# Joint key and value weight loads, token runs of four rows and a newly searched order in a linear-attention and gated-MLP kernel

## The chip, the cores and the metric

The kernel runs on 1 core of one Trainium2 chip. The metric is the time of one execution in microseconds (us) on the device. Executions of one program differ by 0.5 to 3.5 us here, so every comparison below uses several executions and, in the experiments, executions of the kernel before in the same rounds on the same chip. "Span" is the length of the profiled execution as the profile sees it, some 2 us less than the time.

## The reference, cut to what matters

Four layers act on 2048 tokens of 512 values: linear attention, gated MLP, linear attention, gated MLP. Both attentions use the same weights.

```python
def _A_ref(x, wqkv, w_phi, wo):                 # B, S, D = 1, 2048, 512;  H = 32, Dh = 16
    q, k, v = ...                               # x @ wqkv, by heads
    pq = einsum("bhsd,hdf->bhsf", q, w_phi); pk = einsum("bhsd,hdf->bhsf", k, w_phi)
    phi_q = concat([softmax(pq), softmax(-pq)]); phi_k = concat([softmax(pk), softmax(-pk)])
    kv = einsum("bhsf,bhsd->bhfd", phi_k, v);  z = phi_k summed over s
    o = (phi_q @ kv) / (phi_q . z + 1e-6)
    return o.reshape(B, S, D) @ wo
def _B_ref(x, W_gate, W_up, W_down): ...        # relu gate, F = 1376
x = x + _A_ref(layernorm(x), ...);  x = x + _B_ref(layernorm(x), ...)   # and both once more
```

Each attention sums over all tokens (kv, z) before any token can go on. So the kernel has a front, which ends with the first kv product, and a second part. The matrix of the feature map is multiplied into the key weights once ("composed") so that keys come out ready for the softmax.

## The kernel before

The program is a list of operations, each with the tiles that it reads and writes. A table ORDER gives the sequence of operations on each engine and a table CHOICE the engine of those that can run on several. Both were found by a search outside of the kernel. Each engine executes its list strictly in order.

```python
# warm-up: 70 matmuls on a tile of ones, spread by ORDER over the gaps of the first 19 us
for j in range(NWARM):
    op("pe", lambda e: e.matmul(k.pb[3][:, 0:128], k.ones[:], k.ones[:], start=True, stop=True), ...)

# the first loads: 128 KB each, value weights and key weights apart, four token tiles
for ic in range(NC):
    dma("act", ... k.wv_p[:, ic, :] <- A_wqkv[ic * 128:(ic + 1) * 128, 1024:1536])
for ic in range(NC):
    dma("act", ... wk_n[:, ic, :] <- A_wqkv[ic * 128:(ic + 1) * 128, 512:1024])
for t in range(4):
    ldx(t, t + 1)
dma("sp", ... k.phi_c[:] <- A_w_phi)            # the feature map
first = [r("x", 3)]                             # the large loads wait for token tile 3
ldx(4, 8, first); ldx(8, 12, first); ldx(12, 16, first)
...                                             # [cut]
# the end of the front: the kv product is masked and copied out
op("dve", lambda e: e.tensor_tensor(k.kvbd..., pv..., k.mask4..., ALU.mult), ...)   # "kvbd"
```

The softmax here doesn't subtract the row's maximum and nothing guards it: scores larger than these inputs give would overflow.

## Time and profile before

| | before |
|---|---|
| time, median of 3 runs | 379.60 us (379.32 to 379.97) |
| span of the profiled run | 377.4 us |
| statistics of the group of token tile 4 begin | 10.99 us |
| first kvbd copies begin (end of the front) | 53.07 us |
| second kvbd copies begin (third layer) | 236.32 us |

The last three rows are the milestones. From the first kvbd on TensorE is full: its idle time after 50 us, summed over the bracketed waits in its timeline, is 1.2 us. The time is the front, plus the stretch between the two kvbd copies (183.25 us), plus the rest (141.1 us). Three more rows of the timeline of the kernel before (start, duration, engine, line, operation, tiles, count):

```profile
7.60 0.81 PE L725 MATMUL ps<-wv_p,yT 128*128 128x512 bf16 x3
10.99 2.46 DVE L623 BATCH_NORM_STATS2 stats<-x_sb 128x6 f32<-128x512 bf16 x4
6.05 1.48 SPq L543 DMA_DIRECT2D x_sb<-in_A_x_dram  x3
```

The first value projection runs at the fast pitch (three matmuls of 512 columns in 0.81 us). VectorE begins the statistics of the large token group at 10.99. SyncE issues the three large token loads at 6.05, when tile 3 has landed.

### The profile page before, as it was taken

How to read it: one execution, taken by the hardware profiler on the slowest of the kernel's cores; microseconds unless marked ns; L12 is line 12 of the kernel's file. 1: busy time of each engine (PE TensorE's matmuls, PEld its weight loads, DVE VectorE, ACT ScalarE, POOL GpSimd, SP SyncE). 2: the span in 40 equal slices, each digit the busy share in tenths (PEclk: the TensorE clock that was granted, in tenths of full speed). 3: DMA queues.
4: the chain of work that ended last, by engine and by line, in shares of the span. 5: the costliest groups of instructions: out<-in, count | busy, mean ns of one | idle time of the engine just before them, and what ended most of it. 6: DMA issues, size and time to landing. Idle time of an engine off the chain costs nothing.

```text
span 377.4 us, 6882 instructions
## 1 busy us (share of the span) xinstructions
PE 367.7 (97%) x2519; PEld 203.9 (54%) x2565; DVE 276.2 (73%) x607; ACT 227.0 (60%) x463; POOL 130.8 (35%) x234
## 2 busy tenths in 40 slices
PE   6999999999999999999999999999999999999997
PEld 5654555877744454454444446577664454445443
DVE  5999998989968676459799999898984654342323
ACT  3999878765744127874677568584635451653450
POOL 6799941133344001350463577023221201000020
PEclk9999999999999999999999999999999999999999
DMA  7632794313326444310300045335543442142012
GB/s 233 173 76 52 187 240 149 77 33 56 78 43 94 97 64 84 70 30 14 70 2 1 2 81 95 79 63 95 83 83 75 81 86 56 28 71 70 30 42 70
DMA packets 87856, 29.33 MB, mean 78 GB/s; under 512 B 79792, under 2 KB 86800, under 8 KB 87824
## 3 DMA queue, kind: packets, MB, share of 16 engines
q1 hardware_dynamic: 84368, 25.86, 33.7%
q10 hardware_dynamic: 3456, 3.05, 2.5%
q8 instruction: 20, 0.33, 0.4%
q14 instruction: 12, 0.10, 0.1%
HBM read 7.91 MB, written 2.10 MB: 27 GB/s over the span
## 4 chain that ended last, share of the span: by engine, by line
PE 85%; POOL 7%; DVE 3%; issue 2%; ACT 1%; DMA 1%; POOLq 0%; DVEq 0%
PE ps L962 37%; PE ps L1011 20%; PE ps L725 7%; PE ps L942 7%; POOL expk L750 5%; PE ps L822 5%; PE ps L988 3%; PE ps L921 2%; PE ps L787 1%; PE ps L886 1%; DMA hT<-in_A_wqkv_dram 1%; DVE Zk L744 1%; POOL rstd L648 1%; PE ps L868 1%; PE ps L539 0%
## 5 line engine op out<-in xcount | busy, mean ns | idle before, releaser
L962 PE MATMUL ps<-yT,Wgu 128*128 128x512 bf16 (+2 forms) x870 | 150.8, 320 | 0.6
L962 PEld LDWEIGHTS ps<-yT,Wgu 128*128 128x128 bf16 x880 | 78.5, 98 | 58.8 <-ACT expk L970 1.0
L964 ACT ACTIVATE gate_sb<-ps 128x512 bf16<-128x512 f32 (+2 forms) x110 | 50.7, 480 | 55.1 <-PE ps L962 41.8
L1011 PE MATMUL ps<-Wd,hT 128*128 128x512 bf16 (+4 forms) x354 | 79.3, 373 | 0.5
L1011 PEld LDWEIGHTS ps<-Wd,hT 128*128 128x128 bf16 (+1 forms) x363 | 34.6, 98 | 39.5 <-DVE hT L972 0.7
L972 DVE TENSOR_TENSOR hT<-gate_sb,expk 128x512 bf16<-128x512 bf16 (+2 forms) x70 | 23.9, 361 | 30.4 <-ACT expk L970 21.4
L970 ACT ACTIVATE expk<-ps 128x512 bf16<-128x512 f32 (+2 forms) x70 | 32.0, 475 | 22.2 <-PE ps L962 19.5
L710 ACT ACTIVATE sq<-x_sb,nmr 128x512 bf16<-128x512 bf16 x48 | 34.6, 721 | 10.3 <-DVE x_sb L687 6.6
L744 DVE TENSOR_REDUCE Zk<-expk 128x64 f32<-128x1024 bf16 x32 | 38.1, 1203 | 1.0 <-ACT expk L737 0.7
L714 POOL TENSOR_TENSOR rstd<-rv,mone 128x1 f32<-128x1 f32 x32 | 18.6, 589 | 50.2 <-DVE rv L712 50.0
L1013 DVE SCALAR_TENSOR_TENSOR x_sb<-ps,rstd,x_sb 128x512 bf16<-128x512 f32 (+2 forms) x33 | 23.9, 728 | 16.1 <-PE ps L1011 13.5
L942 PE MATMUL ps<-wo_p,oT 128*128 128x512 bf16 x118 | 30.8, 379 | 0.6 <-DVE oT L413 0.3
L975 DVE TENSOR_TENSOR hT<-gate_sb,ps 128x512 bf16<-128x512 bf16 (+2 forms) x40 | 21.7, 544 | 12.6 <-ACT gate_sb L964 6.4
L855 POOL TENSOR_TENSOR expq<-expq,rho 128x256 bf16<-128x256 bf16 x36 | 22.2, 624 | 24.4 <-DVE rho L852 23.7
L847 DVE TENSOR_REDUCE Zq<-expq 128x64 f32<-128x1024 bf16 x24 | 28.8, 1204 | 0.8 <-POOL rho L852 0.5
L687 DVE SCALAR_TENSOR_TENSOR x_sb<-ps,x_sb 128x512 bf16<-128x512 f32 x32 | 21.9, 687 | 8.6 <-PE ps L942 7.8
L750 POOL TENSOR_TENSOR expk<-expk,rZk 128x1024 bf16<-128x1024 bf16 x13 | 25.9, 2005 | 0.6 <-DVE rZk L746 0.6
L755 POOL TENSOR_TENSOR expk<-expk,rZk 128x512 bf16<-128x512 bf16 x17 | 19.1, 1134 | 11.8 <-DVE rZk L746 11.5
L822 PE MATMUL ps<-Wqp,yT 128*128 128x512 bf16 x91 | 22.8, 379 | 0.3
L725 PE MATMUL ps<-Wkp,yT 128*128 128x512 bf16 x84 | 22.0, 379 | 0.2
L725 PE MATMUL ps<-wv_p,yT 128*128 128x512 bf16 x85 | 21.9, 379 | 0.2
L712 POOL TENSOR_SCALAR rv<-rv 128x1 f32<-128x1 f32 x22 | 4.3, 203 | 45.3 <-ACT sq L710 45.3
(126 smaller groups left out, 514.1 us busy)
## 6 DMA issues: line engine op xcount, KB each, us to landing
out_dram<-x_sb ACTq DMA_DIRECT2D x15, 128.0 KB, 1.7
x_sb<-in_A_x_dram SPq DMA_DIRECT2D x3, 512.0 KB, 5.0
Wgu<-in_B_W_up_dram SPq DMA_DIRECT2D x4, 344.0 KB, 5.5
Wgu<-in_B_W_gate_dram SPq DMA_DIRECT2D x4, 344.0 KB, 4.3
Wd<-in_B_W_down_dram SPq DMA_DIRECT2D x5, 256.0 KB, 3.3
yT<-ytile SPq DMA_TRANSPOSE x56, 2.5
qT<-expq SPq DMA_TRANSPOSE x40, 2.5
x_sb<-in_A_x_dram SPq DMA_DIRECT2D x4, 128.0 KB, 3.6
```

The costliest lines, as they stand in the source:

```text
L710: op("act", lambda e: e.activation(k.sq[:], k.x_sb[:, t, :], ACT.Square, scale=-float(D), bias=k.nmr[:, t, :], accum_out=k.rv1[:, t, :]), ...
L725: op("pe", (lambda ic, bank, W: lambda e: e.matmul(k.pb[bank][:], k.yT[:, ic, t * 128:(t + 1) * 128], W[:, ic, :], start=(ic == 0), stop=( ...
L744: op("dve", lambda e: e.tensor_reduce(k.Zk[:, zb, :], k.expk[:, t, :, :, :].rearrange("p g s (h f) -> p (g s h) f", f=16), AX.X, ALU.add), ...
L750: op("pool", lambda e: e.tensor_tensor(kv, kv, k.rZk[:, rb, :].unsqueeze(2).to_broadcast([P, 64, 16]), ALU.mult), [r("expk", t, 0), r("exp ...
L822: op("pe", (lambda ic, bank, tt: lambda e: e.matmul(k.pb[bank][:], k.yT[:, ic, tt * 128:(tt + 1) * 128], k.Wqp[:, ic, :], start=(ic == 0), ...
L847: op("dve", lambda e: e.tensor_reduce(k.Zq[:, b, :], k.expq[:, t, :, :, :].rearrange("p g s (h f) -> p (g s h) f", f=16), AX.X, ALU.add), ...
L942: op("pe", (lambda c, bank: lambda e: e.matmul(k.pb[bank][:], k.oT[:, ob, c, :], k.wo_p[:, c, :], start=(c == 0), stop=(c == NC - 1)))(c, ...
L962: op("pe", (lambda bank, W, ic, fc, Mf: lambda e: e.matmul(k.pb[bank][0:Mf, 0:n], W[:, ic, fc * 128:fc * 128 + Mf], k.yT[:, ic, c0:c0 + n] ...
L964: op("act", (lambda Mf, gb, gs: lambda e: e.activation(k.gate_sb[0:Mf, gs, 0:n], k.pb[gb][0:Mf, 0:n], ACT.Relu))(Mf, gb, gs), [self.RP[gb] ...
L970: op("act", (lambda Mf, ub, up: lambda e: e.activation(up[0:Mf, 0:n], k.pb[ub][0:Mf, 0:n], ACT.Copy))(Mf, ub, up), [self.RP[ub]], ru, 170 ...
L972: op("dve", (lambda Mf, up, gs, u: lambda e: e.tensor_tensor(k.hT[0:Mf, u, 0:n], k.gate_sb[0:Mf, gs, 0:n], up[0:Mf, 0:n], ALU.mult))(Mf, u ...
L1011: op("pe", (lambda fc, Kf, u, c0, bank, m0, m1: lambda e: e.matmul(k.pb[bank][:, m0:m1], k.hT[0:Kf, u, c0:c0 + 128], k.Wd[0:Kf, fc, m0:m1] ...
```

## The change

Its intent: fewer and larger loads at the start (four weight loads of 256 KB in rows of 2 KB in place of eight of 128 KB in rows of 1 KB), the feature map multiplied into the loaded key weights in place, large token loads in packets of 4 KB since each partition holds four neighbouring rows, both queues used for the first tokens, and an order and choice searched for the new loads. All of ORDER and CHOICE differ. They are cut here.

```diff
 ORDER = { ... }      # [cut: every list is new]
 CHOICE = { ... }     # [cut: many small operations change their engine]
-        sb("wv_p", [NC, 512])
+        sb("wkv", [NC, 1024])
+        self.Wkp, self.wv_p = self.wkv[:, :, 0:512], self.wkv[:, :, 512:1024]
-        for ic in range(NC):
-            dma("act", ... k.wv_p[:, ic, :], A_wqkv[ic * 128:(ic + 1) * 128, 1024:1536] ...)
-        for ic in range(NC):
-            dma("act", ... wk_n[:, ic, :], A_wqkv[ic * 128:(ic + 1) * 128, 512:1024] ...)
-        for t in range(4):
-            ldx(t, t + 1)
-        dma("sp", ... k.phi_c ...)
+        def ldkv(eng, ic):
+            dma(eng, ... k.wkv[:, ic, :], A_wqkv[ic * 128:(ic + 1) * 128, 512:1536] ...)
+        ldx("sp", 0, 1)
+        ldx("act", 1, 2)
+        dma("sp", ... k.phi_c ...)
+        ldkv("act", 0)
+        ldkv("act", 1)
+        ldx("sp", 2, 3)
+        ldx("act", 3, 4)
+        ldkv("sp", 2)
+        ldkv("act", 3)
         first = [r("x", 3)]
-        ldx(4, 8, first) ...
+        ldx("sp", 4, 8, first) ...
-        WT, Wn = k.hT[:, 0:4, :], k.hT[:, 8:12, :]
+        WT, Wn = k.hT[:, 0:4, :], k.Wkp
+    def tokens(self, ap, t):
+        g = t // 4
+        v = ap.rearrange("b s d -> (b s) d")[512 * g:512 * g + 512, :]
+        return v.rearrange("(t p) d -> p t d", p=P) if g == 0 else v.rearrange("(p t) d -> p t d", t=4)
```

The stores use tokens() too.

## The prediction

> **What bounds the kernel now.** I read the page first (shares and slices), then the chain of waits, then the windows and the timeline of the first 60 us, because the diff touches the loads at the start.
>
> ```profile
> PE 367.7 (97%) x2519; PEld 203.9 (54%) x2565; DVE 276.2 (73%) x607; ACT 227.0 (60%) x463; POOL 130.8 (35%) x234
> PE   6999999999999999999999999999999999999997
> DVE  5999998989968676459799999898984654342323
> PE 85%; POOL 7%; DVE 3%; issue 2%; ACT 1%; DMA 1%; POOLq 0%; DVEq 0%
> ```
>
> The page says that TensorE bounds everything. For the second part that is true. For the first 53 us I don't take it at its word: the busy time there is full of filler. The timeline of TensorE has 70 matmuls on the tile of ones (the warm-up, L539), spread through the first 19 us in gaps. Real matmuls of 512 columns run at 1.73 us for 8, that is 216 ns each ("160.47 1.73 PE ps L725 x8" in the chain), those of 68 columns at some 33 ns (40 in 1.70 less the tail), those of 128 columns at 56 ns. By these pitches and the matmul counts in the program, the matmuls up to the last of the first key-value accumulation are 46.5 us (3.9 of them warm-up), but that one ends at 53.5. All matmuls together are 364.5 us, so 318.0 come after it; TensorE ends them near 374.4, so they lose about 2.9 us to gaps. The front loses 7.0, plus the 3.9 of filler. So the change can gain in the front, and hardly anywhere else.
>
> Who holds the front? The windows view (busy us in each stretch) and the DVE rows of the timeline:
>
> ```profile
> 2.00:4.00 2.00, 1.47 (x15) 1.20 (x14) 0.42 (x1) 1.21 (x2) 1.55 (x5) 1.00 0.88 286
> 4.00:6.00 2.00, 2.00 (x21) 2.00 (x20) 1.86 (x6) 0.60 (x1) 1.35 (x7) 1.00 0.97 288
> 6.00:8.00 2.00, 1.70 (x19) 1.27 (x19) 1.11 (x4) 0.60 (x1) 0.97 (x4) 1.00 0.87 273
> 8.00:10.00 2.00, 1.09 (x14) 0.68 (x13) 1.88 (x6) 0.94 (x2) 1.83 (x5) 1.00 1.04 352
> ...
> 3.50:8.35 4.85, 4.26 (x39) 3.48 (x40) 3.74 (x10) 1.19 (x2) 2.72 (x12) 1.00 0.92 283
> 8.35:53.10 44.75, 43.37 (x361) 23.94 (x366) 44.13 (x72) 42.05 (x65) 40.30 (x51) 1.00 0.62 136
> ```
> ```profile
> 3.58 0.69 DVE L623 BATCH_NORM_STATS2 stats<-x_sb 128x6 f32<-128x512 bf16 x1 [3.58 <-DMA x_sb<-in_A_x_dram]
> 6.94 0.69 DVE L623 BATCH_NORM_STATS2 stats<-x_sb 128x6 f32<-128x512 bf16 x1 [0.85 <-DMA x_sb<-in_A_x_dram]
> 8.35 0.41 DVE L413 COPY yT<-ps 128x512 bf16<-128x512 bf16 x1
> 16.31 1.22 DVE L744 TENSOR_REDUCE Zk<-expk 128x64 f32<-128x1024 bf16 x1 [0.22 <-ACT expk L737]
> 53.07 0.98 DVE L797 TENSOR_TENSOR kvbd<-ps,mask 128x136 bf16<-128x136 f32 x4
> ```
>
> From 8.35 to 53.1 us VectorE is busy 44.13 of 44.75 us (99%), ScalarE 42.05 (94%), GpSimd 40.30 (90%). The three are balanced, VectorE ahead. The chain names GpSimd's key scaling (L750), but only since the three hand over to each other. The masked copy of the key-value product (kvbd, 53.07) ends this phase and releases the part where TensorE is full. So the front ends when VectorE's list ends: landing of the first token tile (3.58), plus work, plus idle. Idle after 3.58: 1.11 us up to 8.35 (0.85 of it waiting for token tile 2) and 0.62 later. That 1.7 us is nearly all that better loading can win on VectorE, since the 3.58 stays.
>
> [...] the loads of 2 to 8 us (1 KB packets) move 273 to 288 GB/s, but those of 8 to 12 us, 1 KB packets too, 352 to 362. So 1 KB alone isn't the brake. [...] issues cost 0.43 to 0.46 us each on both queues while the engines are already 87 to 97% busy. [...]
>
> **The change part by part.**
> (1) Joint loads: eight weight loads of 128 KB become four of 256 KB: four issues fewer, 4 x 0.45 = 1.8 us of issuing; ScalarE's last weight issue comes at 4.52 now, and near 2.6 (five back to back from 0.80). The bytes (1 MB weights, 0.5 MB tokens, 16 KB feature map) stay. [...]
> (2) Order and split of queues: tokens 0 and 1 head the two queues, so both land near 3.6; tile 2 is third on SyncE behind the tiny map load. Some 0.55 MB are before its end: 2.1 us of start, 0.55 MB / 0.288 = 1.9, and 0.6 of completion (fitted on tile 0): near 4.7 to 5.5. VectorE reaches it after 2.0 us of its list, at 5.6: the wait of 0.85 goes. Tile 3 comes fourth on ScalarE's queue behind 512 KB of weights, with 1.3 MB moved: 2.1 + 4.4 + 0.6 = 7.1, later than now (about 6.0). VectorE wants it near 6.7, so 0.4 us of new wait. The large token loads wait on tile 3, so they start 1 us later[...].
> (3) Moves between engines in the front. VectorE gains two copies of 0.42, one of 0.69, and two small ones of 0.2 each (1.9); it loses two copies of 0.42, the block-diagonal map 0.68 and one token scaling of 0.48 (2.0). The clearing of kvf, 1.06 us on GpSimd, goes to VectorE in the time before 3.58: free. Net -0.1. ScalarE: three of 0.60 out, two of 0.60 and one of 0.81 in: +0.2. GpSimd: kvf and two small ones out, the map in: about -0.3.
> (4) Key weights: the map overwrites the loaded copy. The copies are ordered by the composition itself, so no wait is added. With all weights in near 8.0 us the first exponential could start near 13.5 instead of 15.01, which removes the 0.22 at 16.31 and gives ScalarE slack of over 1 us against +0.2 of work.
> (5) Stores: still rows of 1 KB per partition, now 4 KB apart in memory; same number and size, no change.
> (6) The same 364.5 us of matmuls; the new order after 53 us can only touch the 2.9 us of gaps there. Its 51 moves from GpSimd to VectorE and 33 back are of small pieces in a part where VectorE has room.
> Sum for VectorE's list: idle 1.7 becomes about 0.4 + 0.2 + 0.5 = 1.1, gain 0.6; less work 0.1; so the front ends some 0.7 us earlier, all of which reaches the end, as TensorE is full from there. For the search I add 0.4 in the later gaps, a choice and not a result. 379.6 - 1.1 = 378.5 us.
>
> **The rivals.**
> (a) Loading was hidden: VectorE is at 99%, so taking away its early wait only uncovers the next (tile 3, the large loads, or GpSimd). For it: tile 3 and all that hangs on it come later. Then 379.4 to 380.
> (b) The early phase is really bound by the composed key weights: 15.01 for the first exponential, with TensorE on filler until 14. Then joint loads win 1.5 us in the front for all three engines and the result is near 377.5. Against it: ScalarE starts its exponentials just in time for VectorE (only 0.22 of wait).
> (c) The feature map's 512 packets of 32 bytes, now second in SyncE's queue[...], hold tile 2 and the third weights back by up to 2 us. For it: 653 packets under 512 B pass in 4 to 8 us now, where the rate falls to 138 to 270 GB/s. Then VectorE idles as before and the time is 379.5 to 380.5.
> (d) Larger packets speed the token loads so that later tiles run freely: bounded by the 1.7 us of idle; 377.7.
>
> **Range and chances.** (a) and (c) are about 25% together, (b) and (d) about 30%, the rest about my sum. Beyond 2% would be below 372.0, a gain of 7.6 us: more than all of the front's 7.0 of gaps, so nearly excluded; slower by 2% (387.2) would need a stall that the order tables, made for these loads, don't suggest. The three runs of before span 0.65 us. Range 377.2 to 379.8; faster 0.01, within 2% 0.98, slower 0.01.
>
> **What would show it.** Right: VectorE's first statistics still near 3.6; no wait of 0.85 before the third; a short one before the fourth; kvbd at 52.0 to 52.7 instead of 53.07; the same TensorE time after it. Wrong: VectorE's first start later than 3.8, or kvbd not moved though the waits are gone (then GpSimd or ScalarE sets the end), or the gain arising after 53 us (then the search, not the loads, is the cause). Were the first exponential 1.5 us earlier and kvbd too, rival (b) was right.

Passages on the cost of a packet and on how the queues share the DMA engines are cut, since no trace of this case shows them. The sum came to 1.1 us: 0.6 less idle time of VectorE (1.7 less 0.4, 0.2 and 0.5), 0.1 less work, and 0.4 for the search. Two terms went with the cuts: 0.15 us for larger packets, which wasn't in the sum, and the derivation of the 0.2, VectorE's wait for the first large load, which was put at a landing near 10.3. No trace gave that landing. In the change this load was issued at 7.67 and took 3.7 us to land; in the kernel before, 6.05 and 3.9. That some 0.55 MB pass before tile 2 ends, and 1.3 MB before tile 3 does, are estimates of mine. In the kernel before, the two queues moved 0.30 and 0.27 MB from 2 to 4 us.

## More of the kernel before

From 17 us on, normalized tokens, queries and outputs are transposed by DMA transposes from one on-chip tile to another, issued by SyncE. There are 143 of them.

## The result

The changed kernel took 382.04 us, the median of 4 runs (381.15 to 382.50), against 379.75 (379.32 to 379.97) for the kernel before. Ratios in this document are the mean time of one kernel's fast runs over that of the other's of the same rounds, so not quite the ratio of the medians. Here the ratio is 1.0059, with a 95% interval of 1.0036 to 1.0081. The change costs some 0.6%, where a gain of 0.3% was predicted. The result lies outside of the predicted range.

The page of the changed kernel, shares and chain of waits:

```profile
PE 371.6 (98%) x2565; PEld 203.5 (53%) x2565; DVE 278.9 (73%) x624; ACT 226.8 (60%) x464; POOL 125.7 (33%) x216
PE 92%; ACT 3%; DVE 2%; DMA 2%; issue 0%; ACTq 0%
```

The shares look like those of before; GpSimd's key scaling has left the chain. The page alone doesn't show the loss. Its stretches do (windows view; the length of the stretch, the busy us of PE, PEld, DVE, ACT, POOL, then the granted clock, the DMA share and GB/s):

```profile
6.00:8.00 2.00, 1.15 (x19) 0.83 (x16) 1.20 (x3) 0.60 (x1) 0.47 (x2) 0.99 0.50 190
8.00:10.00 2.00, 2.00 (x9) 0.86 (x9) 1.67 (x5) 1.08 (x2) 2.00 (x4) 0.50 0.69 168
10.00:12.00 2.00, 2.00 (x25) 2.00 (x24) 1.10 (x4) 0.99 (x2) 1.75 (x6) 0.66 0.99 367
```

Between 8 and 10 us TensorE looks full with 9 matmuls, where the kernel before did 14 in 1.09 us, and the granted clock is 0.50. The DMA engines are busy for 50 and 69% of the time between 6 and 10 us. The timeline of the changed kernel (VectorE, then TensorE, then SyncE's issues) shows what waits for what. In brackets is the idle time before the instruction and what ended it.

```profile
6.54 0.69 DVE L633 BATCH_NORM_STATS2 stats<-x_sb 128x6 f32<-128x512 bf16 x1 [0.73 <-DMA x_sb<-in_A_x_dram]
8.30 0.15 DVE L681 TENSOR_SCALAR nrx<-rstd 128x1 f32<-128x1 f32 x1 [0.53 <-POOL rstd L641]
10.78 0.42 DVE L414 COPY yT<-ps 128x512 bf16<-128x512 bf16 x1 [0.50 <-PE ps L691]
12.53 1.87 DVE L633 BATCH_NORM_STATS2 stats<-x_sb 128x6 f32<-128x512 bf16 x3
54.40 1.03 DVE L810 TENSOR_TENSOR kvbd<-ps,mask 128x136 bf16<-128x136 f32 x4
5.60 0.40 PE L691 MATMUL ps<-ident,ytile 128*128 128x128 bf16 x4 [0.83 <-DVE ytile L679]
8.40 1.91 PE L738 MATMUL ps<-wkv,yT 128*128 128x512 bf16 x4
10.10 0.64 PE L691 MATMUL ps<-ident,ytile 128*128 128x128 bf16 x4
7.67 1.29 SPq L543 DMA_DIRECT2D x_sb<-in_A_x_dram  x3
```

VectorE still waits for tile 2 (0.73). It waits for GpSimd (0.53) and for TensorE (0.50, and 0.40 more before a copy at 11.92), and reaches the statistics of tile 4 at 12.53 and not at 10.99. The four matmuls of the first value projection take 1.91 us. TensorE's pace changed within this run: four matmuls of 128 columns took 0.40 us at 5.60 and 0.64 at 10.10. The large loads go out at 7.67, 1.6 us later.

The three milestones sort the loss of this profiled run:

| part | before | change | loss |
|---|---|---|---|
| front, to the first kvbd | 53.07 | 54.40 | 1.33 |
| first to second kvbd | 183.25 | 183.65 | 0.40 |
| second kvbd to the end | 141.1 | 142.55 | 1.45 |

The sum is 3.2 us, the difference of the spans (380.6 less 377.4). In the later part two waits of TensorE are new (waits view: us in total, times, longest):

```profile
PE ps L975 <- ACT expk L983: 0.7, 1, 0.7
PE ps L975 <- DMA yT<-ytile: 0.7, 1, 0.7
```

### The profile page after: what moved, and what is told of

Its sections match the earlier page's. It is cut to its first block, busy times and chain, and to the rows that moved or that the text cites. A ratio compares the mean times of both kernels' runs of the same rounds, so it can differ in the third digit from the quotient of the medians.

```text
span 380.6 us, 6923 instructions
## 1 busy us (share of the span) xinstructions
PE 371.6 (98%) x2565; PEld 203.5 (53%) x2565; DVE 278.9 (73%) x624; ACT 226.8 (60%) x464; POOL 125.7 (33%) x216
## 4 chain that ended last, share of the span: by engine, by line
PE 92%; ACT 3%; DVE 2%; DMA 2%; issue 0%; ACTq 0%
PE ps L975 36%; PE ps L1024 19%; PE ps L738 10%; PE ps L955 7%; PE ps L835 5%; PE ps L1001 3%; PE ps L779 3%; PE ps L800 2%; PE ps L881 2%; PE ps L934 1%; DMA yT<-ytile 1%; PE ps L899 1%; ACT expk L782 1%; DMA x_sb<-in_A_x_dram 1%; PE ps L537 1%; ACT ytile L672 1%
## 5 line engine op out<-in xcount | busy, mean ns | idle before, releaser
L975 PEld LDWEIGHTS ps<-yT,Wgu 128*128 128x128 bf16 x880 | 77.6, 98 | 61.3 <-ACT expk L983 3.2
L1024 PE MATMUL ps<-Wd,hT 128*128 128x512 bf16 (+3 forms) x363 | 80.1, 373 | 0.0
L985 DVE TENSOR_TENSOR hT<-gate_sb,expk 128x512 bf16<-128x512 bf16 (+2 forms) x70 | 24.7, 365 | 32.6 <-ACT expk L983 18.9
L738 PE MATMUL ps<-wkv,yT 128*128 128x512 bf16 x176 | 45.0, 385 | 0.0
L1026 DVE SCALAR_TENSOR_TENSOR x_sb<-ps,rstd,x_sb 128x512 bf16<-128x512 f32 (+2 forms) x33 | 23.8, 723 | 14.4 <-PE ps L1024 11.4
L955 PE MATMUL ps<-wo_p,oT 128*128 128x512 bf16 x128 | 32.5, 379 | 0.3 <-DVE oT L414 0.3
L738 PEld LDWEIGHTS ps<-wkv,yT 128*128 128x128 bf16 x176 | 16.4, 99 | 18.0 <-issue 1.0
L768 POOL TENSOR_TENSOR expk<-expk,rZk 128x512 bf16<-128x512 bf16 x18 | 19.9, 1120 | 6.2 <-DVE rZk L759 6.2
```

What stands on the lines that cost most here:

```text
L738: op("pe", (lambda ic, bank, W: lambda e: e.matmul(k.pb[bank][:], k.yT[:, ic, t * 128:(t + 1) * 128], W[:, ic, :], start=(ic == 0), stop=( ...
L955: op("pe", (lambda c, bank: lambda e: e.matmul(k.pb[bank][:], k.oT[:, ob, c, :], k.wo_p[:, c, :], start=(c == 0), stop=(c == NC - 1)))(c, ...
L975: op("pe", (lambda bank, W, ic, fc, Mf: lambda e: e.matmul(k.pb[bank][0:Mf, 0:n], W[:, ic, fc * 128:fc * 128 + Mf], k.yT[:, ic, c0:c0 + n] ...
L985: op("dve", (lambda Mf, up, gs, u: lambda e: e.tensor_tensor(k.hT[0:Mf, u, 0:n], k.gate_sb[0:Mf, gs, 0:n], up[0:Mf, 0:n], ALU.mult))(Mf, u ...
L1024: op("pe", (lambda fc, Kf, u, c0, bank, m0, m1: lambda e: e.matmul(k.pb[bank][:, m0:m1], k.hT[0:Kf, u, c0:c0 + 128], k.Wd[0:Kf, fc, m0:m1] ...
```

## The experiments

Theory 1 was that the front loses time to the new sequence on TensorE: 29 fillers come at once, then TensorE waits for tokens (0.83 us), and its matmuls are slow when the first value projection comes. The trace of the change shows both paces: matmuls of 512 columns start 427 ns apart at 8.4 us and 216 ns apart at 12.0, and four take 1.91 us or 1.03 us. In that run the granted clock reads 0.50 from 8.0 to 11.3 us and 1.00 from 11.5. That steady work on TensorE brings the fast pitch and a pause loses it was my guess, to be tested by more fillers. Rivals: the late large loads, GpSimd's sequence, the place of the feature map, the packet size, and for the later part the order itself. A later theory, F, is told with its runs. The ratio in each table row is to the kernel before in the same rounds. "v0" is the duration of the four matmuls of the first value projection (for 0.81 of three: fast).

| run | median us (range) | ratio [95%] | v0 | statistics of tile 4 | first kvbd | to second | to end |
|---|---|---|---|---|---|---|---|
| r1_change_again | 381.25 (380.53 to 381.93) | 1.0045 [1.0031, 1.0059] | 1.91 | 12.19 | 54.08 | 183.64 | 142.2 |
| e1_loads_only | 381.84 (379.49 to 382.04) | 1.0052 [1.0033, 1.0072] | 1.91 | 13.35 | 55.24 | 183.28 | 141.2 |
| e2_order_only | 382.05 (381.86 to 382.42) | 1.0068 [1.0056, 1.0080] | 1.57 | 12.32 | 54.22 | 183.66 | 142.2 |
| e3_gate_x2 | 381.62 (380.65 to 382.25) | 1.0055 [1.0040, 1.0069] | 1.91 | 12.45 | 54.65 | 183.64 | 142.0 |
| e4_pool_order | 381.15 (380.44 to 381.85) | 1.0045 [1.0032, 1.0057] | 1.58 | 11.74 | 53.62 | 183.66 | 141.3 |
| e6_warm | 382.04 (380.61 to 383.40) | 1.0073 [1.0052, 1.0094] | 1.03 | 11.20 | 53.32 | 183.65 | 142.5 |
| e8_old_rest | 380.79 (380.58 to 381.08) | 1.0037 [1.0025, 1.0049] | 1.92 | 12.56 | 54.74 | 183.26 | 141.2 |
| e10_mended | 383.87 (383.36 to 385.08) | 1.0122 [1.0106, 1.0138] | 1.03 | 10.42 | 55.04 | 185.10 | 141.2 |
| e11_map_last | 381.64 (380.53 to 382.14) | 1.0043 [1.0026, 1.0060] | slow | 12.10 | 54.01 | 183.65 | 142.1 |
| e15_rows_1kb | 382.12 (381.40 to 382.73) | 1.0059 [1.0042, 1.0075] | fast | 11.56 | 53.62 | 183.66 | 142.2 |
| e13_pool_old_rest | 379.89 (379.20 to 381.46) | 1.0008 [0.9987, 1.0029] | fast | 10.94 | 52.83 | 183.29 | 141.2 |
| e12_best | 382.31 (381.60 to 382.56) | 1.0060 [1.0045, 1.0076] | fast | 10.83 | 52.75 | 186.21 | 141.1 |
| e16_warm_moved | 379.58 (379.25 to 380.11) | 1.0002 [0.9989, 1.0015] | 1.03 | 11.63 | 53.63 | 183.26 | 141.2 |
| e17_pad_17 | 382.72 (382.56 to 384.14) | 1.0098 [1.0083, 1.0113] | 1.03 | 11.09 | 54.25 | 185.40 | 141.2 |
| e18_before_pad_17 | 381.55 (380.80 to 381.76) | 1.0050 [1.0038, 1.0062] | 1.39 | 10.58 | 52.86 | 185.03 | 141.1 |
| e19_change_pad_17 | 385.47 (382.49 to 385.94) | 1.0139 [1.0113, 1.0165] | 1.03 | 11.01 | 54.16 | 185.00 | 141.4 |

The kernel before took 379.57, 379.32, 379.81 and 379.47 us (medians of 11 runs each) in the four sets of rounds. All runs gave correct results. The last five columns come from one profiled run each, while the median is of 4 to 6. The two don't always move together, and where they part the median decides.

When the fast pitch begins can be read in each trace from the distance between the starts of TensorE's matmuls. In the kernel before, the fast pitch begins at 6.3 us. In the change's profile it came by 5.7, was lost at 8.0 and came back at 11.4. Nine more profiles have the change's front with its own fillers, some with one small edit: in four the fast pitch begins at 4.3 to 5.9 us (e13, e15, e17, e19), in five only at 9.5 to 11.0 (r1, e3, e4, e8, e11). So one and the same list can be fast or slow at the first value projection (e4 and e13 have the same lists up to the first kvbd). The four runs with more fillers before it (e6, e10, e12, e16) had the fast pitch in time. This fits theory 1, but that the bunched fillers are the reason isn't shown: the list of before with the new loads (e1) had the fast pitch only at 10.7.

### The change repeated, and its two halves

```diff
 r1_change_again:  (no edit)
 e1_loads_only:    the change
-  ORDER and CHOICE of the change
+  those of before, with the new load issues in place of the old
 e2_order_only:    the kernel before
-  ORDER and CHOICE of before
+  those of the change, with the old load issues in place of the new
```

> The changed kernel unaltered, for a second sample: 381.2 to 382.6 us, ratio to before 1.004 to 1.008. The profiled run of it had TensorE's granted clock at 0.50 and 0.66 between 8 and 12 us; if that is a chance event of one run, this profile shows 1.00 there and the time is hardly less; if the dip belongs to the kernel, it is there again.

> New loads and layout with the instruction order and engine choice of the kernel before. Theory A (the new loads bring token tile 3 in at 7.7 us instead of 6.0, and with it the release of the large token loads, so the front ends later): 381 to 382 us, the kv copy at 54 us or later. Theory B (the searched order is at fault, above all in the second part): 379.4 to 380.2 us, kv copy at 53 us.

> Loads and layout of before with the new instruction order and engine choice. Theory A: 379 to 380 us. Theory B: 381 to 382.5 us, with the same gaps on TensorE after 60 us as the changed kernel (1.0 us more than before).

The loss repeats (1.0045). The windows view of the repeat shows a clock of 1.00 at 8 to 10 us, where the same four matmuls took 1.91 us. The column also reads 1.00 from 2 to 6 us in the kernel before, where the fillers start 107 ns apart, against 56 later. So the pitch has to be read and not this column.

Both halves are slower alone, by as much as the whole: 1.0052 and 1.0068. So neither loads nor order is an improvement that the other spoils, and the costs don't add. Each half has an order made for other landings and loses in the front (55.24 and 54.22). But in both profiles the fast pitch also came late (10.7 and 10.1 us), and one of the six runs with the new loads alone took 379.49 us, so how much the landings cost isn't shown. The extra time after the first kvbd (183.65 and 142.2) is in the run with the new order and old loads, and not in the run with new loads and the old order. It comes with the order and not with the loads; the section "Stream length alone" narrows this.

### The large loads released earlier

```diff
-        first = [r("x", 3)]
+        first = [r("x", 2)]
```

> The changed kernel, but the large token loads and the query weights wait for token tile 2 (landed 6.5 us) instead of tile 3 (7.7 us). If the late release and the hole in the transfers between 7 and 8.3 us hold the front (theory A1): 0.7 to 1.2 us faster than the changed kernel of the same rounds. If VectorE's early order holds it (theory A2: no wait for the large loads is seen at 12.5 us): no change within 0.4 us.

SyncE issued the large loads at 5.50 us, 1.8 to 2.2 us before the change's, and the first kvbd came at 54.65. The late large loads aren't what holds the front. They are hidden behind other waits.

### GpSimd's sequence

```diff
 ORDER["pool"], by names
-L0 rv1 2, L0 rstd 0, L0 rstd 2
+L0 rstd 0, L0 rv1 2, L0 rstd 2
```

> The changed kernel with one swap on GpSimd: the inverse root of token tile 0 before the variance of tile 2. If VectorE's wait for it before the statistics of tile 3 (0.53 us) is on the path (theory A2): statistics of tile 3 near 7.2 instead of 7.9, tile 4 and kv copy 0.5 us earlier, time 0.5 us less. If VectorE is held later by TensorE's copies anyway (theory C): no change in the kv copy, time the same within 0.3.

In the change the reciprocal deviation of tile 0 stands behind a step of tile 2 on GpSimd, which waits for tile 2, and VectorE waits 0.53 us for it. With the two swapped that wait is gone, the statistics of tile 3 begin at 7.44 and not at 7.86 to 8.37, and the first kvbd is 0.5 us earlier than in the repeat (its fast pitch came 0.8 us earlier too). The medians (381.15 and 381.25) don't separate. Alone its effect on the time isn't shown.

### TensorE kept busy

```diff
+ 17 more filler matmuls on the tile of ones where TensorE waits, between 4.8 and 8.3 us; two moved
```

> The changed kernel with 18 more filler matmuls (and two moved) in the waits of TensorE between 4.8 and 8.3 us, nothing else. Theory C (the new early order leaves TensorE idle at 4.8 to 5.6 us and again while it waits for weights, so its matmuls still run at the slow pitch, 1.91 us for the four of the first value projection instead of 1.03, and VectorE's copies wait behind them): the four take 1.03 us, the statistics of tile 4 begin near 11.3 instead of 12.2 to 12.5, the kv copy comes some 0.9 us earlier, time 0.9 us under the changed kernel. Rival (the late weights alone hold the value projection): pitch or no pitch, statistics of tile 4 not before 12.0 and time the same.

From the timeline:

```profile
8.18 1.03 PE L738 MATMUL ps<-wkv,yT 128*128 128x512 bf16 x4
53.32 1.02 DVE L810 TENSOR_TENSOR kvbd<-ps,mask 128x136 bf16<-128x136 f32 x4
```

The effect is there: the projection takes 1.03 us, and the first kvbd comes 0.8 us before the repeat's and 1.1 before the change's. Yet the median didn't improve (382.04, range 2.8 us). That contradiction led to theory F below. Its profiled run shows no longer stretch between the copies (183.65), so there the loss of the other runs isn't seen.

### The old order after the front

```diff
 ORDER, CHOICE: the change's for all that starts before the first kvbd
-  the change's for the rest
+  those of before for the rest
```

> The changed kernel up to the first kv copy, from there the order and engine choice of the kernel before. Theory B2 (the new order loses 0.4 us between the two kv copies and 1.0 us after the second one, independent of the loads): kv copy at 54.2, from there 183.3 to the second one and 141.1 to the end, as before; time about 380.3 to 380.8. Rival (those 1.4 us come from the loads, the layout of the stores or the state that the front leaves): 381.3 to 382.

The later stretches return to 183.26 and 141.2, as in before. The median fell by only 0.46 against the repeat, since this run's front was slow (v0 1.92, kvbd 54.74).

### Everything mended at once: a miss

```diff
+ fillers as above, GpSimd's swap, large loads after tile 2, old order after the front
+ VectorE: statistics of tiles 4 and 5 moved ahead of work for tiles 2 and 3
```

> All mends at once: filler, GpSimd swap, large token loads released by tile 2, statistics of tiles 4 and 5 moved into VectorE's two waits, old order after the kv copy. If the kv copy follows the statistics of tile 4 by 41.9 us less the 1.3 us moved ahead, as in all five profiles so far, and the filler works: kv copy at 51.5 to 52.5, time 378 to 379.2, faster than the kernel before. If something else holds the front (GpSimd or ScalarE): kv copy at 53 or later, time 379.5 or more.

This was the slowest of its rounds, also between the copies (185.10; it holds the 17 fillers too, see theory F). The statistics of tile 4 came at 10.42, but TensorE then waited 1.15 us for the tile that they had overtaken, and kvbd came at 55.04. From there to kvbd it took 44.6 us, where runs that keep VectorE's list take 41.9 to 42.2: the constant holds only for the list.

### The feature map last, and token rows of 1 KB

```diff
 e11_map_last, SyncE's queue
-x0, map, x2, third weights
+x0, x2, third weights, map
 e15_rows_1kb
-v.rearrange("(t p) d -> p t d", p=P) if g == 0 else v.rearrange("(p t) d -> p t d", t=4)
+v.rearrange("(t p) d -> p t d", p=P)
```

> The change with the feature map's load (512 small packets) moved from second to last place of the first four loads on SyncE's queue. If the small packets hold back what follows (rival c of the prediction): tile 2 lands before 6.1 us (6.54 in the change) and the third weights before 7.1 (7.46), and the first kvbd copy comes 0.3 to 0.5 us earlier than the change's 54.1 to 54.4 unless GpSimd's block-diagonal map, which then waits for the load until about 7.5, takes it back. If the map's place doesn't matter: tile 2 lands at 6.4 or later and the time is the change's, 381.3 to 382.

> The change with the old token layout (1 KB rows in the three large token loads and in the stores), all else kept. If 4 KB packets buy something: the large loads take at least 0.4 us more from issue to landing than the change's 3.7, 4.2 and 5.5 to 6, and the first kvbd copy and the time are later by as much if that is on the path. If not: landings within 0.3 us, kvbd at 54.1 to 54.5, time 381.2 to 382.0, so the packet size neither helps nor hurts.

With the map last, tile 2 landed at 4.2 us (issued 1.26, 2.9 to landing) against 6.0 in the repeat and 6.5 in the change. That part of rival (c) of the prediction is right. But tile 3 then landed at 7.9 and the map at 8.8, and the time is the change's (1.0043). With 1 KB rows the three large loads took 3.8, 4.8 and 5.7 us to landing, against 3.7, 4.7 and 6.3 in the change and 3.2, 4.3 and 6.1 in its repeat. The time is the change's. The packet size of the tokens does nothing that these runs can show. The second run also had a fast v0 without any edit there, and so its kvbd at 53.62: whether the fast pitch comes in time for v0 varies from run to run (4.3 to 5.9 us in four of the nine profiles above, 9.5 to 11.0 in five).

### Two mends, and the same with fillers

```diff
 e13_pool_old_rest:  GpSimd's swap and the old order after the front
 e12_best:           the same
+  17 more filler matmuls between 4.8 and 8.3 us
```

> The change with GpSimd's reciprocal of tile 0 ahead of tile 2's (as in the pool-order run) and, after the first key-value copy, the order of before (as in the old-rest run). If the two mends add up: first kvbd copy near 53.7 (53.62 and 54.74 in the two single runs), then 183.3 to the second copy and 141.2 to the end, so a span near 378.4 and a time near 380.2. If GpSimd's order is without effect on the time, as the pool-order run's median (381.15 against 381.25 of the change) suggests, it stays at 380.8 like the old-rest run.

> The run above plus 18 filler matmuls on TensorE where it waits between 4.8 and 8.3 us. Warm-up theory: the four matmuls of the first value projection take 1.03 us and not 1.6 to 1.9, the statistics of tile 4 begin near 11.0, first kvbd copy at 52.8 to 53.2, span near 377.6, time near 379.5: the loss is gone. Rival (the filler helps the profiled run only, or its wake costs as much later): the time is 380.2 or more, no better than the run without filler.

(Here and for the run before with fillers, the text on record says 18. It was 17: 2582 weight loads against 2565.) Without the fillers no loss clear of noise is left: 1.0008, with runs from 379.20 to 381.46, of which the profiled one was the fastest. With them it is back: 1.0060. The first and second kvbd of the run without, then of the run with fillers:

```profile
52.83 1.01 DVE L818 TENSOR_TENSOR kvbd<-ps,mask 128x136 bf16<-128x136 f32 x4
236.12 1.10 DVE L818 TENSOR_TENSOR kvbd<-ps,mask 128x136 bf16<-128x136 f32 x4
```
```profile
52.75 1.01 DVE L818 TENSOR_TENSOR kvbd<-ps,mask 128x136 bf16<-128x136 f32 x4
238.96 1.09 DVE L818 TENSOR_TENSOR kvbd<-ps,mask 128x136 bf16<-128x136 f32 x4
```

Both start the second part at the same moment, and from there all five engines have the same instructions in the same order. Still the run with fillers loses 2.9 us before the second kvbd. Its waits of TensorE between 52 and 240 us:

```profile
PE ps L963 <- DMA oT<-osb: 1.2, 2, 0.9
PE ps L746 <- DMA yT<-ytile: 0.9, 1, 0.9
PE ps L907 <- DVE expk L422: 0.5, 1, 0.5
PE ps L1009 <- DMA yT<-ytile: 0.2, 1, 0.2
PE ps L889 <- DVE qT L829: 0.2, 1, 0.2
```

The run without fillers has only the two waits for VectorE, at the same size. The three new lines, four waits in all, are for DMA transposes. One place is near 92 us. SyncE's queue in the run without fillers, then in the run with them, and last a row of the latter's DMA queues from 94 to 98 us (packets, MB, share):

```profile
90.72 5.13 SPq L729 DMA_TRANSPOSE yT<-ytile  x4
```
```profile
90.70 6.12 SPq L729 DMA_TRANSPOSE yT<-ytile  x4
```
```profile
q8 instruction: 1, 0.02, 2.3%
```

The same four transposes took 1.0 us more (6.12 against 5.13) in the run in which one packet of a queue called "instruction" passes among them. In the run without fillers that packet comes after 98 us. The page of the changed kernel lists 20 such packets on queue q8, 0.33 MB or 16 KB each. From one such packet to the next TensorE starts 124 to 126 weight loads on average in every run (124.7 in the kernel before, 124.8 in the change), so with the matmuls some 250 instructions, although the packets come 8 to 30 us apart. So I take these packets for fetches of TensorE's instructions, and call them so below. It is an inference from the queue's name and this count. **Theory F:** a filler in the front shifts all later fetches in the stream, and a fetch that meets a transpose on which TensorE waits costs about a microsecond, as here (1.0).

### Stream length alone

```diff
 e16_warm_moved:     e12_best
-  17 of the fillers at 17 to 19 us (so the count is that of e13_pool_old_rest)
 e17_pad_17:         e13_pool_old_rest
+  17 tiny matmuls (8 columns) among the fillers at 18 us
 e18_before_pad_17:  the kernel before
+  the same 17 tiny matmuls near 19 us
 e19_change_pad_17:  the change
+  the same 17 tiny matmuls near 18.7 us
```

> The run with two mends and fillers again, but its 17 extra fillers are taken from those at 17 to 19 us, so the number of instructions after the front is that of the two-mends run. Theory F (fetch places): first kvbd copy at 52.7 to 53.0, 183.3 us to the second (not 186.2), TensorE idle after 50 us near 1.0 us, time 379.3 to 379.9. Rival (warm fillers cost time later by themselves): 186 us between the copies and a time near 382.

> The two-mends run with 17 tiny matmuls (8 columns) added among the fillers at 18 us, where TensorE waits anyway: they warm nothing, only the stream is longer by as many instructions as in the run with 17 more fillers. Theory F: first kvbd copy at 52.8 to 53.2, but some 186 us to the second copy, TensorE waiting for DMA transposes near 97, 118, 137 and 233 us, time 381.6 to 382.5. Rival: 183.3 between the copies and the time of the two-mends run, 379.9.

> The kernel before with the same 17 tiny matmuls among its last fillers near 19 us. Theory F: its order after 53 us is nearly that of the two-mends run, so it too meets the fetches: first kvbd copy at 53.1, 185 to 186.5 us to the second (183.25 in before), time 381 to 382.3. Rival: 379.6 as without them.

> The change itself with the same 17 tiny matmuls near 18.7 us. Theory F for its later loss: the wait of 0.5 to 0.7 us for a transpose near 315 us goes or changes place, others may come; the time differs from the change's 381.3 to 382.0 by more than 0.5 us in either direction, with the first kvbd copy still at 54.1 to 54.4. If its later loss is of the order and not of the fetches, the time from the second copy to the end stays 142.2 to 142.6.

With the fillers moved and the count kept, the stretch is 183.26 us again and the ratio 1.0002. So the fillers don't cost time later by themselves. (Its first kvbd, 53.63, missed the expected 52.7 to 53.0: TensorE waited 0.43 us at 8 us in this run.) The cleanest test is the kernel before, where the front didn't suffer (first kvbd 52.86, second 237.89) and the time rose by 2.1 us, with a wait that was not there before, here in TensorE's timeline:

```profile
232.30 1.04 PE L725 MATMUL ps<-Wkp,yT 128*128 128x512 bf16 x4 [0.77 <-DMA yT<-ytile]
```

The run of two mends with the same pad has the like at the same place:

```profile
234.06 1.90 PE L746 MATMUL ps<-wkv,yT 128*128 128x512 bf16 x8 [1.03 <-DMA yT<-ytile]
```

It lost 2.1 us between the copies, and also 1.4 in the front, where its pad delayed a value projection by 0.8 us. That part isn't theory F's. (TensorE had the fast pitch by 5.8 us in this run, four matmuls of 128 columns in 0.40 us, so tiny ones at 18 us had none to bring.) The rival fell: by the medians, 17 matmuls of 8 columns near 18 us cost 2.1 us in one kernel and 2.8 in the other. For the change itself, the pad made the stretch after the second kvbd shorter (141.4 against 142.2 to 142.6) and the one before longer (185.0 against 183.65). Its expectation had said that a loss of the order alone would stay at 142.2 to 142.6. So the change's loss at the end isn't of the order alone: it is of where that order meets the fetches, if theory F holds. In the change, the place is this (SyncE's queue, TensorE's timeline, and the DMA queues from 312 to 316 us):

```profile
312.55 2.28 SPq L871 DMA_TRANSPOSE qT<-expq  x1
315.63 1.04 PE L975 MATMUL ps<-yT,Wgu 128*128 128x512 bf16 x4 [0.68 <-DMA yT<-ytile]
```
```profile
q8 instruction: 1, 0.02, 2.0%
```

One transpose holds the queue for 2.28 us where 1.27 is usual, and a fetch lies in the stretch. The other new wait, 0.72 us for ScalarE near 363 us, follows a fetch too. The changed kernel's store issues on ScalarE's queue, the wait that follows, and the same two issues in the run with GpSimd's swap:

```profile
360.42 2.01 ACTq L1035 DMA_DIRECT2D out_dram<-x_sb  x2
363.12 2.12 PE L975 MATMUL ps<-yT,Wgu 128*128 128x512 bf16 x9 [0.72 <-ACT expk L983]
```
```profile
359.31 0.82 ACTq L1035 DMA_DIRECT2D out_dram<-x_sb  x2
```

A fetch passes at 360.74 in the changed kernel, and ScalarE's next piece starts only when the issues are over (they end at 362.43, it starts at 362.47). The two waits are 1.4 of the 1.45 us lost there. The run with GpSimd's swap has the change's order, but for the swap, and its stream length, and only other times, and there the stretch after the second kvbd was 141.3. That stream length sets the time is shown by the four runs. That the fetch is what slows the transpose wasn't tested by itself, but all 18 kept traces agree. Of their 2574 on-chip transposes, 2312 have no 16 KB packet while they hold the queue, and none of these holds it for more than 1.64 us, though 153 meet one of the smaller packets (8 KB) of a second instruction queue, q14. Of the 262 that have one, 137 hold it longer, up to 2.72 us. The 284 store issues without such a packet took 0.65 us at most; six of the 22 with one took 1.46 to 1.64, in the very six profiles that have the wait near 363 us. The padded change also ran between 382.5 and 385.9, and its profiled run was the fastest of the six, so what the others lost isn't seen.

No version beat the kernel before. The best two, 1.0002 and 1.0008, equal it.

## Why the prediction was wrong

It named the bound rightly. VectorE's list sets the front: from the statistics of tile 4 to the first kvbd it takes 42.1 us in before, 41.9 in the change, and 41.9 to 42.2 in every run that keeps one of the two lists of VectorE and adds no pad after it. It was also right that no rival would move the time by 2%. The rest failed in these steps.

**Part (2), landings.** Tile 2 was put at 4.7 to 5.5 us and VectorE's wait of 0.85 was to go. It landed at 6.5, and 0.73 of wait stayed. In the repeat it landed at 6.0 and the timeline shows no wait for it, and the loss was there all the same, so this wait isn't what cost the time. The estimate took the map's load for "tiny" by its bytes. The run with the map last has tile 2 at 4.2, so the map ahead of it cost 1.8 us of landing against the repeat, 0.46 of it the place of its issue. The prediction had that as rival (c), too low in weight. Tile 3 landed at 7.7 in place of 7.1, so the large loads waited longer, but releasing them early gained nothing.

**Parts (2) to (4), the sum of VectorE's idle time.** It was to fall from 1.7 to 1.1 us. From 3.66 to 12.53 alone it is 0.73 + 0.53 + 0.50 + 0.40 = 2.16 us, and the new list also puts some 0.4 us more work before the statistics of tile 4 (busy 6.62 us from 3.66 to 12.53, against 6.26 from 3.58 to 10.99 in before). The step that failed was to treat VectorE as waiting for loads only. Of the four waits one is for a load. One is for GpSimd, whose list holds tile 0's value behind tile 2's. Two are for TensorE, whose v0 ran at half pitch (1.91 us in place of 1.03), as it did, at least in part, in six of the ten profiles with this front and its own fillers. The prediction counted fillers as free, never looked at where the change puts them, and took 56 ns for every matmul of 128 columns. In before those up to 6.3 us start 107 ns apart: 39 of them, so by my estimate 2.0 of the 7.0 us that it counted as lost in the front are the slow pitch. (Of the 0.2 us of wait put down for the large loads there was none at tile 4.) The first exponential came at 15.45 us and not near 13.5 (15.01 in before).

**Part (6), the search.** I gave it 0.4 us of gain in the later gaps, put at 2.9 us where the waits in the timeline sum to 1.2, and "the same TensorE time after it". In the profiled run the time from the first kvbd to the end rose from 324.3 to 326.2 us. Of the 1.9 us, 0.4 comes between the copies in every unpadded run with the new order; TensorE's waits don't grow there, and its cause stays open. The rest comes after the second, from the two waits at fetches above. The view that the later part is full and so safe was wrong. In before six transposes that meet a fetch hold the queue for 1.66 to 2.36 us too, but none on which TensorE then waits, and a new order or stream length deals again (185.0 to 185.4 us between the copies in the three padded runs).

**Part (1) and rival (d), packets.** The saving of issues happened but met nothing that waited for it. The 4 KB packets made no difference, as the 1 KB run shows. Against part (4)'s view that overwriting the weights in place adds no wait, and against part (5), the stores, I found nothing.

**The range** was set from the front's known gaps and the spread of the kernel before. It had no term for a loss in the second part, and little for a front that gets worse.

Where the 2 us are: the mends of GpSimd's list and of the later order together bring the ratio from 1.0045 to 1.0008, with intervals that don't overlap, though neither alone does more than 0.1%. In the profile of the first run with both the fast pitch came early (4.3 us), so it may have a part in that. Which share is the pitch's isn't settled, since it varies from run to run: in the profile a fast v0 is worth 0.5 to 1.1 us of front.

## What to carry to other kernels

Before trusting a new order on a tuned kernel, follow each engine's list through the first microseconds: a load, a reciprocal and a burst of fillers that each look free can hold up one another, since every list is strictly in order (VectorE's wait of 0.53 us here hung on the place of one reciprocal in GpSimd's). When one engine is full to the end, look also at what must arrive just in time for it; there a change of a few instructions far away can cost as much as the change under test (17 tiny matmuls cost 2.1 and 2.8 us here, the change 2.3). So compare variants of the same stream length, or try several lengths, before you credit a difference of half a percent to an edit.
